# Scale copies tied to their transposes, first slots from nine tiles, one gather per f-tile, in a one-core attention and mixture-of-experts kernel

## The chip, the cores and the metric

The kernel runs on one core of a Trainium2 chip. The metric is the device time of one launch in microseconds; lower is better. Times of several runs are given as their median.

## What is computed

Linear attention (4 batch entries, 8 heads, 576 rows, 64 columns), then a dense gated feed-forward layer on the 2304 x 512 result, then a layer of 8 experts of which each row uses one:

```python
x = x @ w_gate * sigmoid(x @ w_gate) * (x @ w_val) @ w_out      # 512 -> 1536 -> 512
e_idx = np.argmax(x @ w_gate2, axis=1)                          # the row's expert
for e in range(8):
    mask = e_idx == e
    h = np.maximum(x[mask] @ w1[e], 0.0)                        # 512 -> 1024
    out[mask] = gate_w[mask, None] * eom[mask, e, None] * (h @ w2[e])
```

All of it is float32. The kernel splits every matmul operand into a high part and a low part and multiplies three times (high by high, high by low, low by high).

## The kernel before

The 2304 rows are 18 tiles of 128, handled by the dense layer in six blocks of 384 rows (three tiles). Blocks 0 to 3 run one after the other, mixed with attention. Blocks 4 and 5 share their first products in `pair` (lines 693 to 753). What is left of block 5 then runs alone: a loop over its 12 f-tiles (lines 1457 to 1474), here called **block 5's stretch**. For f-tile f it takes the low part of the hidden tile (`h5`, line 684, on VectorE), the split of the output weights (`cut`, line 641: the high part on ScalarE, the low part on GpSimd) and nine matmuls (`o_tiles`, line 577, trace lines 582 to 584). The third matmul of each group of three reads the hidden tile's low part. Every helper's instructions carry the helper's line, so `h5` and `cut` both show as L642 (ScalarE) and L643 (VectorE or GpSimd): 128x384 is a hidden tile, 128x512 are weights.

After a block, `post_x2` (line 909) writes its rows to the DRAM buffer `x2d`. `post(n)` (line 1366) lists what follows for block n: transposes (L920) with a copy back (L921), the logits (L928, L935), and the routing of its rows, `route_a` and `route_b`, the first of which writes each row's scale into four more columns of `x2d`. `route_early` (line 1037) and `slot_map` (line 1005) then pick rows for the first 8 slot tiles (two **quads** of four tiles, each with one expert) from the tiles known so far, `EARLY_T` = 12, which are blocks 0 to 3. These lists are worked off in small pieces between the large matmuls (`fine` during `pair`, `fill` later). Where the routing code goes through a recorder, its instructions show as L879 or, called directly, L876.

`rows` (line 1404) takes four gather buffers and `gather_q(0)` fetches the rows of the first quad by four indirect DMAs on GpSimd's queue (`fetch`, L1165). `xt_q(0, t)` (line 1193), called at f = 8 to 11, transposes gathered tile t on TensorE (L1179), copies the transpose's high part out on ScalarE (L1181), takes the low part on VectorE (L876) and copies the rows' scale to `SCQ` on VectorE (L1197). Then `quads` (line 1238) runs four quads; `split_q` (L1210, L1213) splits their weights. Single slots follow (`moe2`), four of them as long as the routing needs no more.

Within one engine instructions run in the order that a scheduler gave them. It may place an instruction far ahead of its place in the code as soon as its inputs are named as ready. `tie(x)` (line 901) bounds that: x is placed behind the last matmul kept in `state["pe"]`. It is an order, not a wait.

Of the kernel before, what the change touches and what calls it, by code (L numbers as in the profile page):

```python
# [19 lines left out]
P = 128  # L20
NT, DM, DFF = B * S, H * D, 1536
# [9 lines left out]
NEQ = 2  # L31
# [153 lines left out]
def kernel(ctx, tc, qT, kT, v1, wphi, w1cat, wlog, mw1, mw2, consts, out):  # L185
    nc = tc.nc
    PE, ACT, DVE, POOL, SP = nc.tensor, nc.scalar, nc.vector, nc.gpsimd, nc.sync
# [14 lines left out]
    def buf(n):  # L202
        a = ar.take(n)
        return A[:, a:a + n]
# [5 lines left out]
    o = 0  # L210
# [3 lines left out]
    ident = cv["ident"]  # L214
# [16 lines left out]
    SCQ = buf(8)  # L231
# [43 lines left out]
    state = {"n": 0, "banks": [0, 1, 2, 3, 4, 5, 6, 7], "rd": 0}  # L275
# [613 lines left out]
    def bc(ap, n):  # L889
        return ap.rearrange("p (j o) -> p j o", o=1).to_broadcast([P, ap.shape[1], n])  # L890

    def bm(ap, n):
        return ap.rearrange("p (o e) -> p o e", o=1).to_broadcast([P, n, ap.shape[1]])

    def v3(ap, j, e):
        return ap[:, :j * e].rearrange("p (j e) -> p j e", e=e)

    def tt(out_, a, b, op):
        return DV.tensor_tensor(out=out_, in0=a, in1=b, op=op)

    def tie(x):
        if x is not None:
            tc.add_manual_dep(x.ins, state["pe"].name, mybir.DependencyInfo(
                mybir.DependencyClass.NoSync, mybir.DependencyReason.SCHED_ONLY), reason="pace")

    def rsum(out_, a):
        DV.tensor_reduce(out=out_, in_=a, axis=AX.X, op=ALU.add)

    def post_x2(n, t):
        i = 3 * n + t  # L910
        x2 = X2[t]
        ACT.activation(x2, PS[:, (OUT5 if n == 5 else OUTB)[t], :], AF.Copy, scale=0.5)
        SP.dma_start(out=x2d[i * P:(i + 1) * P, 0:DM], in_=x2)
# [66 lines left out]
    def excl(out_, a):  # L980
        w = v3(T1, 8, 8)
        tt(w, cv["m8"].rearrange("p (e f) -> p e f", f=8), bm(a, 8), ALU.mult)
        rsum(out_, w)

    def pick(out_, a, nt):
        w = v3(T1, nt, 8)
        tt(w, OH[:, 0:nt, :], bm(a, nt), ALU.mult)
        rsum(out_, w)
# [40 lines left out]
        tt(T3[:, a:s0 + ns], EXF[:, a:s0 + ns], EXF[:, a - 2:s0 + ns - 2], ALU.not_equal)  # L1029
        DV.tensor_copy(CHI[:, a:s0 + ns], T3[:, a:s0 + ns])  # L1030

    EARLY_T = 12

    def every4(name):
        return cv[name][:, 3:16:4]

    def route_early():

        nt = EARLY_T
        q, tk, ge, r = S1[:, 0:nt], S2[:, 0:nt], S3[:, 0:nt], RK[:, 0:nt]  # L1040

        def counts():
            w = v3(T1, 8, 4)
            tie(tt(w, bc(NB, 4), bm(every4("thge"), 8), ALU.is_ge))
            rsum(E1, w)
            excl(E2, E1)

        def taken():
            tie(DV.tensor_scalar(out=E3, in0=E2, scalar1=-1.0, scalar2=float(NEQ), op0=ALU.mult, op1=ALU.add))
            DV.scalar_tensor_tensor(out=TKE, in0=E3, scalar=0.0, in1=E1, op0=ALU.max, op1=ALU.min)  # L1050
            tt(E4, E2, TKE, ALU.add)
            DV.tensor_scalar(out=TKE, in0=TKE, scalar1=4.0, scalar2=None, op0=ALU.mult)
            DV.tensor_scalar(out=E2, in0=E2, scalar1=4.0, scalar2=None, op0=ALU.mult)

        def picks():
            pick(q, E2, nt)
            pick(tk, TKE, nt)

        def place():
            tie(tt(ge, r, tk, ALU.is_ge))  # L1060
            tt(q, q, r, ALU.add)
            DV.scalar_tensor_tensor(out=q, in0=ge, scalar=1000.0, in1=q, op0=ALU.mult, op1=ALU.add)

        return [(totals, (nt,)), (counts, ()), (taken, ()), (experts, (E4, NEQ, 0)), (picks, ()),
                (place, ()), (slot_columns, (q, nt, 4 * NEQ, True))]
# [68 lines left out]
    XG = []  # L1134
# [28 lines left out]
    def fetch(col, i):  # L1163
        rows = EARLY_T * P if col < 4 * NEQ else NT
        return POOL.indirect_dma_start(out=XG[i], out_offset=None, in_=x2d[0:rows, :],  # L1165
                                       in_offset=IndirectOffsetOnAxis(ap=IDX[:, col:col + 1], axis=0),
                                       bounds_check=rows - 1, oob_is_err=False)
# [8 lines left out]
    def turn_x(i, hi, lo):  # L1176
        ps = PS[:, XB, :]
        for k in range(4):
            PE.transpose(ps[:, k * P:(k + 1) * P], XG[i][:, k * P:(k + 1) * P], ident)  # L1179
        p3 = ps.rearrange("p (k t) -> p k t", k=4)  # L1180
        ACT.activation(hi, p3, AF.Copy)  # L1181
        tt(lo, p3, hi.bitcast(F32), ALU.subtract)
# [1 line left out]
    def xt(s):  # L1184
        turn_x(s % 4, XCH[s % 2], XCL[s % 2])

    def gather_q(q):
        for t in range(4):
            g = fetch(4 * q + t, t)
            if q == 0:  # L1190
                tie(g)

    def xt_q(q, t):
        ts_ = slice(t * P, (t + 1) * P)
        turn_x(t, XQH[:, :, ts_], XQL[:, :, ts_])
        o = 4 * (q % 2) + t
        DVE.tensor_copy(SCQ[:, o:o + 1], XG[t][:, DM:DM + 1])  # L1197

    def split_q(g):
        q, c = divmod(g, 16)  # L1200
# [165 lines left out]
    def post(n):  # L1366
        return [(post_log, (n, t)) for t in range(3)] + [(f, (n,)) for f in (post_mm, post_sum, route_a, route_b)]
# [15 lines left out]
    def fine(n):  # L1383
        first = True
        while n > 0:
            if not small:
                if not todo:
                    return
                small.extend(ops(*todo.pop(0)))
                continue  # L1390
            e, f = small.pop(0)
            while True:
                x = f()
                if first and e in (DVE, ACT):
                    tie(x)
                    first = False
                if e is not PE or not small or small[0][0] is not PE:
                    break
                e, f = small.pop(0)
            n -= 1 if e is not None or f is idle else 2  # L1400
# [3 lines left out]
    def rows():  # L1404
        t = ov.tile([P, OVN], F32, name="ov_gather", tag="ov")
        for s in range(4):
            XG.append(t[:, s * 520:s * 520 + ROW])
            DVE.memset(XG[s], 0.0)
        gather_q(0)

    todo, xs = [], []
    for n in range(1, NBLK - 2):
# [30 lines left out]
    def rest(f, g):  # L1443
        if g == 2:
            if f == 0:
                for i in range(3):
                    post_x2(3, i)
                todo.extend(post(3) + route_early() + [(slot_map, (EARLY_T, 4 * NEQ, 0, True))])
        if f or g == 2:
            fine(2)  # L1450

# [5 lines left out]
    for f in range(NFT):  # L1457
        if f >= 2:
            h5(f)
        w = slot(3 * NFT + f)  # L1460
        cut(w, WR[f][2], POOL)
        mm = o_tiles(5, f, range(3), OUT5, G5(f), w)
        if f == 8:
            state["pe"] = mm.ins
        if f == 1:
            o_tiles(4, NFT - 1, range(3), OUTB, (GH[1], GL[1]), W2)
            for i in range(3):
                post_x2(4, i)
            load_w(0, 1)
            rows()  # L1470
        if f >= 2:
            fill(1)
        if f >= 8:
            xt_q(0, f - 8)
# [62 lines left out]
```

## Time and profile before

| what | us |
|---|---|
| time, median of 3 runs | 899.76 (899.32 to 900.19) |
| the profiled execution's own time | 898.41 |
| its span in the profile | 896.6 |
| TensorE busy in the span | 868.4 (97%) |
| mean granted clock | 0.992 |

The profile is of one execution. Its span runs from the first to the last instruction; the profiled execution's own time is 1.8 us longer, and 1.35 us under the median of the three runs. The granted clock is TensorE's, as a share of full speed. Times inside the trace are us from the span's start.

### The profile page before, as it was taken

The numbers are of one execution on the slowest core, as the hardware profiler recorded it, in microseconds if no ns is written. First come the engines' busy times: TensorE is split into PE (matmuls) and PEld (weight loads), VectorE is DVE, ScalarE is ACT, GpSimd is POOL, SyncE is SP. The second block draws the span as 40 slices with busy tenths as digits, with TensorE's granted clock in tenths as the row PEclk, the third lists the DMA queues.
The fourth block names the chain that finished last, engine by engine and source line by source line (L and its number), as shares of the span: only waits on it lengthen the run. The fifth ranks groups of instructions, "written<-read, shape, count | busy, mean of one in ns | idle before, by whom it ended". The sixth has DMA issues, their size and how long they took to land. (4 is left out here: it accounts for less than half of the span.)

```text
span 896.6 us, 17294 instructions
## 1 busy us (share of the span) xinstructions
PE 868.4 (97%) x6849; PEld 754.1 (84%) x6851; DVE 522.8 (58%) x1028; ACT 475.5 (53%) x921; POOL 387.2 (43%) x339
## 2 busy tenths in 40 slices
PE   8899999999999999999999999996999999999995
PEld 6789988989998988888899999995678888888784
DVE  6999785543335634546556676672677444344693
ACT  6867776535453544544465555562433434344783
POOL 1667989445543433443456566545301212120120
PEclk9999999999999999999999999998999999999998
DMA  8757544200020011110000000009411234010650
GB/s 239 225 174 219 164 129 133 63 16 1 2 77 17 27 43 43 28 51 1 1 2 1 36 1 1 1 4 361 137 41 27 75 112 165 17 55 1 225 215 11
DMA packets 20362, 70.41 MB, mean 79 GB/s; under 512 B 5294, under 2 KB 5550, under 8 KB 18992
## 3 DMA queue, kind: packets, MB, share of 16 engines
q1 hardware_dynamic: 16704, 59.21, 20.7%
q0 software_dynamic: 3200, 9.48, 3.3%
q8 instruction: 55, 0.90, 0.4%
q10 hardware_dynamic: 368, 0.53, 0.2%
q14 instruction: 35, 0.29, 0.1%
HBM read 72.84 MB, written 10.00 MB: 92 GB/s over the span
## 5 line engine op out<-in xcount | busy, mean ns | idle before, releaser
L529 POOL TENSOR_TENSOR arena_r<-arena,arena_r 128x512 fp32r<-128x512 f32 x143 | 184.3, 1293 | 176.0 <-ACT arena_r L525 175.8
L525 ACT ACTIVATE arena_r<-arena 128x512 fp32r<-128x512 f32 x143 | 90.1, 631 | 156.6 <-PE banks L546 96.8
L545 PE MATMUL banks<-arena_r 128*128 128x384 f32 x384 | 135.0, 352 | 0.0
L547 PE MATMUL banks<-arena_r 128*128 128x384 f32 x384 | 129.2, 336 | 0.0
L546 PE MATMUL banks<-arena_r 128*128 128x384 f32 x384 | 129.2, 336 | 0.0
L584 PE MATMUL banks<-arena_r 128*128 128x512 f32 x216 | 86.9, 402 | 7.9 <-DVE arena_r L643 7.9
L1210 ACT ACTIVATE arena_r<-arena 128x512 fp32r<-128x512 f32 x64 | 40.3, 632 | 97.8 <-PE banks L1221 46.9
L1213 DVE TENSOR_TENSOR arena_r<-arena,arena_r 128x512 fp32r<-128x512 f32 x64 | 45.1, 705 | 78.8 <-ACT arena_r L1210 78.6
L582 PE MATMUL banks<-arena_r 128*128 128x512 f32 x216 | 88.8, 411 | 0.0
L583 PE MATMUL banks<-arena_r 128*128 128x512 f32 x216 | 85.9, 398 | 0.0
L642 ACT ACTIVATE arena_r<-arena 128x512 fp32r<-128x512 f32 (+1 forms) x73 | 44.0, 612 | 64.9 <-PE banks L677 34.6
L545 PEld LDWEIGHTS banks<-arena_r 128*128 128x128 f32 x384 | 72.1, 188 | 5.0 <-issue 1.2
L546 PEld LDWEIGHTS banks<-arena_r 128*128 128x128 f32 x384 | 72.3, 188 | 0.6
L547 PEld LDWEIGHTS banks<-arena_r 128*128 128x128 f32 x384 | 72.1, 188 | 0.1
L1170 POOL DMA_INDIRECT out_dram<-arena x20 | 22.9, 1143 | 109.8 <-ACT arena L1265 39.1
L643 POOL TENSOR_TENSOR arena_r<-arena,arena_r 128x512 fp32r<-128x512 f32 x37 | 48.1, 1303 | 41.0 <-ACT arena_r L642 40.1
L557 DVE SCALAR_TENSOR_TENSOR arena<-arena,banks 128x384 f32<-128x384 f32 x48 | 26.5, 551 | 67.0 <-ACT arena L554 66.9
L1165 POOL DMA_INDIRECT ov_gather<-x2d,arena x20 | 21.7, 1086 | 99.1 <-PE banks L1179 96.5
L324 DVE TENSOR_REDUCE arena<-banks 128x6 f32<-128x768 f32 x48 | 45.8, 954 | 30.6 <-PE banks L316 29.7
L584 PEld LDWEIGHTS banks<-arena_r 128*128 128x128 f32 x216 | 41.2, 191 | 17.8 <-DVE arena_r L643 8.8
L316 PEld LDWEIGHTS banks<-arena 64*128 64x128 f32 x576 | 38.3, 187 | 16.8 <-issue 9.4
L1234 PE MATMUL banks<-arena_r 128*128 128x512 f32 x128 | 51.0, 399 | 0.0
(165 smaller groups left out, 2091.8 us busy)
## 6 DMA issues: line engine op xcount, KB each, us to landing
arena<-mw SPq DMA_DIRECT2D x16, 2048.0 KB, 8.0
ov_conv<-w1cat SPq DMA_DIRECT2D x24, 512.0 KB, 4.5
arena<-w1cat SPq DMA_DIRECT2D x12, 512.0 KB, 3.6
arena<-v SPq DMA_DIRECT2D x16, 325.0 KB, 3.3
x2d<-arena SPq DMA_DIRECT2D x18, 256.0 KB, 2.1
arena<-qT SPq DMA_DIRECT2D x15, 288.0 KB, 3.7
arena<-kT SPq DMA_DIRECT2D x15, 288.0 KB, 4.3
ov_gather<-x2d,arena POOLq DMA_INDIRECT x20, 3.7
```

The source lines that it names most:

```text
L324: DVE.tensor_reduce(out=MX, in_=ps, axis=AX.X, op=ALU.max, apply_absolute_value=True)
L525: ACT.activation(WH[i % 4], WR[f][w], AF.Copy)
L529: POOL.tensor_tensor(out=WL[i % 4], in0=WR[f][w], in1=WH[i % 4].bitcast(F32), op=ALU.subtract)
L545: PE.matmul(ps, wh[:, c], xh, start=(k == 0), stop=False)
L546: PE.matmul(ps, wh[:, c], xl, start=False, stop=False)
L547: state["pe"] = PE.matmul(ps, wl[:, c], xh, start=False, stop=(k == 3)).ins
L582: PE.matmul(ps, gh[:, ts_], woh, start=(f == 0), stop=False)
L583: PE.matmul(ps, gh[:, ts_], wol, start=False, stop=False)
L584: mm = PE.matmul(ps, gl[:, ts_], woh, start=False, stop=(f == NFT - 1))
L643: eng.tensor_tensor(out=w[1], in0=src, in1=w[0].bitcast(F32), op=ALU.subtract)
L1213: DVE.tensor_tensor(out=l, in0=src, in1=h.bitcast(F32), op=ALU.subtract)
L1234: PE.matmul(ps, h[:, c], wh, start=(f == 0), stop=False)
```

## The change

The scale copies are tied to their transposes, the first 8 slots are chosen from nine tiles (blocks 0 to 2), so that block 3's `post` can come after the choice, the memsets of the gather buffers are tied, and the four gathers of the first quad come one at a time behind f-tiles 2 to 5.

```diff
-    EARLY_T = 12
+    EARLY_T = 9
...
     def turn_x(i, hi, lo):
         ps = PS[:, XB, :]
         for k in range(4):
-            PE.transpose(ps[:, k * P:(k + 1) * P], XG[i][:, k * P:(k + 1) * P], ident)
+            mm = PE.transpose(ps[:, k * P:(k + 1) * P], XG[i][:, k * P:(k + 1) * P], ident)
+        state["pe"] = mm.ins
...
-    def gather_q(q):
-        for t in range(4):
-            g = fetch(4 * q + t, t)
-            if q == 0:
-                tie(g)
+    def gather_q(q, ts=range(4)):
+        for t in ts:
+            tie(fetch(4 * q + t, t))
...
-        DVE.tensor_copy(SCQ[:, o:o + 1], XG[t][:, DM:DM + 1])
+        tie(DVE.tensor_copy(SCQ[:, o:o + 1], XG[t][:, DM:DM + 1]))
...
-            DVE.memset(XG[s], 0.0)
-        gather_q(0)
+            tie(DVE.memset(XG[s], 0.0))
...
-                todo.extend(post(3) + route_early() + [(slot_map, (EARLY_T, 4 * NEQ, 0, True))])
+                todo.extend(route_early() + [(slot_map, (EARLY_T, 4 * NEQ, 0, True))] + post(3))
...
-        if f == 8:
-            state["pe"] = mm.ins
+        state["pe"] = mm.ins
+        if 2 <= f < 6:
+            gather_q(0, [f - 2])
```

What it moves, by engine. The lines of the changed kernel are one lower from `gather_q` on (L1197 becomes L1196), and L1181 becomes L1182.

VectorE, block 5's stretch, before: the scale copies (L1197) stand among the hidden tiles' low parts (L643) and the copies of block 4's transposes (L921).

```order
L643 TENSOR_TENSOR arena_r<-arena,arena_r 128x384 x2
L1197 COPY arena<-ov_gather 128x1 x2
L643 TENSOR_TENSOR arena_r<-arena,arena_r 128x384
L1197 COPY arena<-ov_gather 128x1
L921 COPY arena<-banks 128x512
L1197 COPY arena<-ov_gather 128x1
L643 TENSOR_TENSOR arena_r<-arena,arena_r 128x384
```

The same place in the changed kernel:

```order
L1407 MEMSET ov_gather 128x516 x4
L643 TENSOR_TENSOR arena_r<-arena,arena_r 128x384 x2
L921 COPY arena<-banks 128x512
L643 TENSOR_TENSOR arena_r<-arena,arena_r 128x384
L921 COPY arena<-banks 128x512
L643 TENSOR_TENSOR arena_r<-arena,arena_r 128x384
```

The scale copies are gone from here; each now stands next to the low part of its own transpose, some 25 rows later. The first two L643 of the first fence are f-tiles 2 and 3, the next are 4 and 5; in the second fence the first two are 3 and 4, and f-tile 5 follows one L921.

GpSimd, the same stretch: the gathers (L1165) against the low parts of the output weights (L643).

```order
-L643 TENSOR_TENSOR arena_r<-arena,arena_r 128x512 x6
-L1165 DMA ov_gather<-x2d,arena 128x516 x4
 L643 TENSOR_TENSOR arena_r<-arena,arena_r 128x512 x7
+L1165 DMA ov_gather<-x2d,arena 128x516
+L643 TENSOR_TENSOR arena_r<-arena,arena_r 128x512
+L1165 DMA ov_gather<-x2d,arena 128x516
+L643 TENSOR_TENSOR arena_r<-arena,arena_r 128x512
+L1165 DMA ov_gather<-x2d,arena 128x516
+L643 TENSOR_TENSOR arena_r<-arena,arena_r 128x512
+L1165 DMA ov_gather<-x2d,arena 128x516
+L643 TENSOR_TENSOR arena_r<-arena,arena_r 128x512 x3
```

Of seven weight splits (f-tiles 5 to 11) that stood behind all four gathers, f-tile 5's now stands ahead of them, and those of 6, 7 and 8 stand each behind one gather.

ScalarE, the end of the stretch and the start of the quads, in the changed kernel; in the kernel before, the first three L1210 (weights of the first quad) stood among the L1181.

```order
L1182 ACTIVATE arena_r<-banks 128x4x128
L642 ACTIVATE arena_r<-arena 128x384
L1182 ACTIVATE arena_r<-banks 128x4x128 x2
L912 ACTIVATE arena<-banks 128x512 x3
L1182 ACTIVATE arena_r<-banks 128x4x128
L1209 ACTIVATE arena_r<-arena 128x512 x4
```

The first quad's first three weight splits now come behind the last transpose's copy.

## Rows read from the trace of the kernel before

**Rows 1.** Page, 40 slices of the span: TensorE busy in tenths, granted clock.

```profile
PE   8899999999999999999999999996999999999995
PEclk9999999999999999999999999998999999999998
```

**Rows 2.** Waits of TensorE, whole span, longest: us in total, times, longest.

```profile
PE banks L584 <- DVE arena_r L643: 7.9, 2, 5.6
```

**Rows 3.** Timeline, TensorE: start, us, engine, line, operation, count, [idle before <-releaser].

```profile
612.80 0.60 PE L920 MATMUL banks<-arena 128*128 128x128 f32 x4
...
615.31 0.60 PE L920 MATMUL banks<-arena 128*128 128x128 f32 x4
...
615.98 0.40 PE L583 MATMUL banks<-arena_r 128*128 128x512 f32 x1
621.99 0.80 PE L584 MATMUL banks<-arena_r 128*128 128x512 f32 x1 [5.61 <-DVE arena_r L643]
...
625.25 0.81 PE L920 MATMUL banks<-arena 128*128 128x128 f32 x4
...
628.85 0.66 PE L584 MATMUL banks<-arena_r 128*128 128x512 f32 x1 [2.32 <-DVE arena_r L643]
...
632.00 1.04 PE L928 MATMUL banks<-arena 128*32 128x384 f32 x8
```

**Rows 4.** Timeline, VectorE, the same stretch.

```profile
621.29 0.15 DVE L1197 COPY arena<-ov_gather 128x1 f32<-128x1 f32 x1 [4.54 <-DMA ov_gather<-x2d,arena]
621.37 0.56 DVE L643 TENSOR_TENSOR arena_r<-arena,arena_r 128x384 fp32r<-128x384 f32 x1
...
628.15 0.15 DVE L1197 COPY arena<-ov_gather 128x1 f32<-128x1 f32 x1 [2.96 <-DMA ov_gather<-x2d,arena]
628.23 0.56 DVE L643 TENSOR_TENSOR arena_r<-arena,arena_r 128x384 fp32r<-128x384 f32 x1
```

**Rows 5.** Windows: stretch, length, busy time by engine, then granted clock, DMA share, GB/s.

```profile
622.00:625.20 3.20, 3.20 (x7) 2.13 (x7) 0.77 (x2) 0.25 (x1) 0.00 (x0) 0.50 0.93 392
```

**Rows 6.** Timeline, TensorE: routing's small matmuls at the pair's end.

```profile
606.04 0.45 PE L879 MATMUL banks<-arena 128*128 128x24 bf16 x12 [0.49 <-DVE arena L879]
606.34 0.48 PE L584 MATMUL banks<-arena_r 128*128 128x512 f32 x1
```

**Rows 7.** Timeline, TensorE, VectorE and ScalarE, from the transposes to the first quad.

```profile
639.74 0.61 ACT L1210 ACTIVATE arena_r<-arena 128x512 fp32r<-128x512 f32 x1
...
643.09 0.66 PE L1179 MATMUL banks<-arena,ov_gather 128*128 128x128 f32 x4 [0.25 <-DVE arena_r L876]
...
648.08 0.15 DVE L1197 COPY arena<-ov_gather 128x1 f32<-128x1 f32 x1 [2.06 <-DMA ov_gather<-x2d,arena]
...
648.88 0.66 PE L1179 MATMUL banks<-arena,ov_gather 128*128 128x128 f32 x4 [0.56 <-DVE arena_r L876]
...
650.22 0.73 PE L1220 MATMUL banks<-arena_r 128*128 128x512 f32 x2 [0.25 <-ACT arena_r L1181]
651.28 0.50 PE L1221 MATMUL banks<-arena_r 128*128 128x512 f32 x1 [0.33 <-DVE arena_r L876]
```

**Rows 8.** GpSimd: one weight split, all 20 gathers (ns min/median/max), all gathers to landing.

```profile
608.94 1.46 POOL L643 TENSOR_TENSOR arena_r<-arena,arena_r 128x512 fp32r<-128x512 f32 x1 [3.02 <-ACT arena_r L642]
...
L1165 POOL DMA_INDIRECT ov_gather<-x2d,arena x20: 995/1002/1612, 610.6 to 786.8; - x20
...
DMA to landing us min/median/max: 2.7/3.7/13.4
```

**Rows 9.** Timeline: stores to x2d on SyncE, a copy behind one; single slots' outputs.

```profile
610.22 1.90 SPq L913 DMA_DIRECT2D x2d<-arena  x3
...
647.60 1.71 SPq L913 DMA_DIRECT2D x2d<-arena  x3
...
652.23 0.69 DVE L921 COPY arena<-banks 128x512 f32<-128x512 f32 x1 [1.00 <-DMA x2d<-arena]
...
L1305 ACT ACTIVATE arena<-banks,ov_gather x4: 687/688/689, 855.2 to 887.4; 128x512 f32<-128x512 f32 x4
```

## The prediction

> **What bounds the kernel now.** I read the page's slices first. TensorE is busy in nearly every slice, and one slice stands out: the 28th of 40, about 605 to 627 us, at 6 tenths; in the slice behind it the granted clock falls [rows 1]. So TensorE sets the end, and only a gap of TensorE is worth anything. The table of waits names the gap: the matmul of L584, two waits, 7.9 us, released by VectorE's L643 [rows 2]. The timeline places both in block 5's stretch: L584 waits 5.61 us at 621.99 and 2.32 us at 628.85 [rows 3]. L584 is the matmul that reads the hidden tile's low part.
>
> Why was L643 late? On VectorE's timeline it starts at 621.37 right behind the scale copy L1197 of 621.29, which had itself waited 4.54 us for a gather to land; the second L643 (628.23) stands behind a copy that waited 2.96 us [rows 4]. The copies need 0.15 us and nobody needs them there. They stand ahead of the low parts of f-tiles 4 and 5 in VectorE's order, so TensorE waited for a gather it had no use for yet. Every gap has a second price: at 622.0 to 625.2 TensorE is busy all the time at a granted clock of 0.50, that is at 1.2 GHz instead of 2.4 [rows 5].
>
> **The change part by part.** *Copies behind their transposes.* The order of the changed kernel shows no scale copy among the low parts of f-tiles 2 to 8. I price this by starts on TensorE. With nothing in the way, transposes, nine matmuls and the next transposes take 615.31 - 612.80 = 2.51 us. The next two rounds took 625.25 - 615.31 = 9.94 and 632.00 - 625.25 = 6.75 us [rows 3]. Above 2.51 each that is 7.43 + 4.24 = **11.7 us**: 7.9 of waiting, the other 3.7 from the low clock. I expect both to go.
>
> *The routing's end.* The changed kernel makes the slot map during the pair and ends the pair with block 3's own ranking. Before, twelve small matmuls waited 0.49 us and ran from 606.04 to 606.34; six such, without a wait, should take half of the 0.30 [rows 6]. Gain 0.49 + 0.30 - 0.15 = **0.6 us**. Nine tiles instead of twelve also save three small matmuls, nothing that counts. Block 3's transposes move from the pair's start to its end, with as many rows as before; the pair's large matmuls cover them.
>
> *The transposes and the first quad.* Here TensorE waited 0.25, 0.56, 0.25 and 0.33 us [rows 7]. Three of the four were released by L876, the low parts of the transposes, behind scale copies of the next quad (one waited 2.06 us for its gather) and behind weight splits. Those 0.25 + 0.56 + 0.33 = 1.14 us should go, as the next quad's copies are tied too. Against this, the first quad's weight splits now come behind the last transpose's copy on ScalarE, and the first takes 0.61 us [rows 7], partly beside VectorE's last low part. I take a net gain of **0.7 us**; the ends are a loss of 0.6 (all of the split added, no wait gone) and a gain of 1.4 (all four waits gone).
>
> *Gathers between weight splits.* On GpSimd a split takes 1.46 us here, and a gather 1.0, the longest 1.61 [rows 8]; the splits of f-tiles 6, 7 and 8 now wait for one gather each, f-tile 9's for the fourth. From 608.94 + 1.46 = 610.4 on: f-tile 5's split to 611.9, then a gather and a split each round, at most 2.8 us with their gaps, so f-tile 8's ends at about 620.3 and f-tile 9's at 623. TensorE, at 2.51 us a round, reads them at 617.8 + 3 x 2.51 = 625.3 and at 627.9. Cost nothing, with 5 us of cover; gone when the four gathers take over 1.0 + 5 / 4 = 2.3 us each, and from there on every further us of a gather costs up to 4.
>
> *Will the gathers be there?* They start at about 612, 615, 618 and 620.5, later than before, but the transposes come earlier: without the gaps the first is due at 628.3 and the others 2.5 apart. The longest landing of any gather was 13.4 us (median 3.7) [rows 8], and those were issued under the same weight loads. By the worst, 620.5 + 13.4 = 633.9 against 635.8. Covered, by 2 us at the worst.
>
> *What now stands first on VectorE.* The low part of f-tile 5 comes behind the copy L921 of block 4's first transpose, which must wait until the store of these rows to `x2d` has landed. One such copy waited for its store until 652.23 [rows 9], 4.6 us after the first issue of its group at 647.6. Issued at 610.2 [rows 9], a store that slow is in by 614.8. TensorE's third matmul of f-tile 5 is due at 617.8 + 0.9 = 618.7 (0.9 from the round's L920 to it, as from 615.31 past 615.98 [rows 3]); less the copy, 0.69 [rows 9], and the low part, 0.56 [rows 4], the store must be in by 617.4. Covered, by 2.6 us. The memsets stay on VectorE and only close up.
>
> Sum: 11.7 + 0.6 + 0.7 = **13.0 us**. Against the profiled execution's own 898.4 that is 885.4; that execution is 1.35 us under the median of the runs shown, so on the median 899.76 - 13.0 = **886.8 us**.
>
> **The rivals.** *A late transfer takes the copies' place.* If the first store landed as slowly as the slowest gather, 610.2 + 13.4 = 623.6, the low part of f-tile 5 would be 6.2 us late at the same spot; if the last gather slipped by 5 us, TensorE would wait 3 at its transposes. For it: the DMA share is 0.93 while the weights load [rows 5], and the second quad's loads come earlier now, as the weights they overwrite are released earlier. Against it: stores are issued ahead of the weight loads, and each limit above used the worst row. Time: 3 to 6.2 us back and up to 2 of clock, 890 to 895. Chance 0.09.
>
> *Gathers that GpSimd builds slowly beside a busy VectorE.* Before, the four gathers were issued while VectorE stood idle; now it works. By rows the nearest is the longest of the 20, 1.61 us, with VectorE busy: below the 2.3 that decides, no loss. At 5 us each the four would cost 4 x (5 - 2.3) = 10.8 us, and 897.6 is the time. The Trainium skill speaks for it: "SBUF — State Buffer", section "SBUF: two separate sides", says that GpSimd cannot write the descriptors of its DMAs while VectorE holds the port pair that they share, and tells of a DMA that took about five times as long beside VectorE copies. By that factor, as an estimate from that page, a gather would take the 5 us just priced. The 1.61 us row [rows 8] does not agree with such a factor here, so the chance is 0.03.
>
> *Slower: an early quad runs empty.* The first two quads need two experts with at least 512 rows each among the first nine tiles (or one with 1024). If only one quad is filled, the other still runs, on nothing, and up to 512 rows come back as four more single slots. Four singles' outputs lie 887.4 - 855.2 = 32.2 us apart over three steps [rows 9], 10.7 each, so +43 - 13 = +30, about 930 us. Against it: nine tiles are 1152 rows, exactly two batch entries of 576, and with the reference's inputs each entry goes to one expert, 576 and 576, which fills the same two quads that twelve tiles fill. Chance 0.01.
>
> *The copies weren't it.* Each named wait could hide a second one that ends just after (a gap of L643 by ScalarE, say). ScalarE's high parts of these tiles were ready and the low part started 0.08 us after the copy [rows 4], so there is little room: 0.02, with a gain under 2 us.
>
> **How the numbers follow.** Forecast 0.85, late transfer 0.09, slow gathers 0.03, the copies weren't it 0.02, empty quad 0.01. The likeliest is the forecast, 886.8. Its own ends: the transposes' 0.6 loss instead of 0.7 gain gives 888.1, the 1.4 gain gives 886.1, and measuring against the profiled execution instead of the median gives another 1.4 down, 884.7. The range takes in the nearer end of the late transfer: 884.4 to 890.2. A measurement of this kernel tells 0.2% (1.8 us) from no change. Faster by more than that: forecast, late transfer and most of the slow gathers, 0.97; within it 0.015; slower 0.015.
>
> **What would show it.** In the changed kernel's waits, L584 behind L643 is gone; between the transposes L920 of block 5's stretch lie 2.5 us throughout, the granted clock stays 1.00 and no slice of TensorE falls to 6 before the last ones. The first L1179 starts some 12 us earlier, at about 627.8, and its gather has landed by then. VectorE has no wait for a gather ahead of an L643 of f-tiles 4 to 8. Wrong would be: L584 still waiting for L643, now with an L921 behind a store ahead of it; L1179 waiting for a gather; a weight split of GpSimd releasing L583; or more than four single slots.

## The result, and the profile after

The changed kernel takes **885.78 us** (median of 4 runs, 885.21 to 885.95), the kernel before 899.54 us beside it (4 runs, 899.03 to 900.19): a ratio of 0.9846, 95% interval 0.9828 to 0.9863. Predicted were 886.8 us, 884.4 to 890.2, a gain of 13.0; by the medians the gain is 13.8 us, by the two profiled executions 12.6. The profiled execution took 885.83 us with a span of 884.1; before, 898.41 and 896.6.

The page of the changed kernel, TensorE and its granted clock in 40 slices, to lay beside [rows 1]: the hole of the 28th slice and the fall of the clock in it are gone. (Both digits stand in the same slice of [rows 1]; the prediction read the fall into the slice behind.)

```profile
PE   8989999999999999999999999999999999999995
PEclk9999999999999999999999999999999999999998
```

The waits of TensorE in the changed kernel, the longest and the new one (us in total, times, longest). L584 [rows 2] no longer stands there; a new wait of 0.8 us ahead of the first quad does.

```profile
PE banks L387 <- DVE arena L327: 2.8, 4, 0.9
...
PE banks L1219 <- ACT arena_r L1209: 0.8, 1, 0.8
```

The timeline of TensorE over block 5's stretch, to lay beside [rows 3]. From L920 to L920 it is 2.51 and 2.52 us, and from the last L920 to L928 2.62; of these rounds the two with waits took 9.94 and 6.75 before.

```profile
613.14 0.60 PE L920 MATMUL banks<-arena 128*128 128x128 f32 x4
...
615.65 0.60 PE L920 MATMUL banks<-arena 128*128 128x128 f32 x4
...
618.17 0.60 PE L920 MATMUL banks<-arena 128*128 128x128 f32 x4
...
620.79 0.85 PE L928 MATMUL banks<-arena 128*32 128x384 f32 x8
...
628.73 0.64 PE L1179 MATMUL banks<-arena,ov_gather 128*128 128x128 f32 x4
...
638.19 0.50 PE L1219 MATMUL banks<-arena_r 128*128 128x512 f32 x1 [0.82 <-ACT arena_r L1209]
```

The timeline of VectorE, to lay beside [rows 4]: no scale copy stands ahead of the low parts any more, and the first one (now L1196) comes at 630.25 without a wait.

```profile
614.14 0.68 DVE L921 COPY arena<-banks 128x512 f32<-128x512 f32 x1
616.18 0.56 DVE L643 TENSOR_TENSOR arena_r<-arena,arena_r 128x384 fp32r<-128x384 f32 x1 [1.35 <-PE banks L584]
616.66 0.68 DVE L921 COPY arena<-banks 128x512 f32<-128x512 f32 x1
...
630.25 0.14 DVE L1196 COPY arena<-ov_gather 128x1 f32<-128x1 f32 x1
```

The windows of the changed kernel (stretch, length, busy time of TensorE, weight loads, VectorE, ScalarE, GpSimd; then granted clock, DMA share, GB/s), to lay beside [rows 5]: TensorE is busy all the time at a granted clock of 1.00, which is 2.4 GHz.

```profile
615.00:625.00 10.00, 10.00 (x56) 7.59 (x55) 3.81 (x8) 4.18 (x8) 7.56 (x8) 1.00 1.01 416
```

To see where the 12.5 us between the two spans lie, two more rows of the kernel before are wanted: a marker at the program's start and the first transposes of a gathered tile.

```profile
55.22 0.94 PE L316 MATMUL banks<-arena 64*128 64x128 f32 x12 [0.81 <-DVE arena L327]
...
640.12 0.64 PE L1179 MATMUL banks<-arena,ov_gather 128*128 128x128 f32 x4
```

In the changed kernel the marker stands at 55.65.

| Stretch | before | after | saved | predicted |
|---|---|---|---|---|
| start to the marker L316 | 55.22 | 55.65 | -0.43 | 0 |
| marker to the first L920 of block 5's stretch (pair, routing's end) | 557.58 | 557.49 | 0.09 | 0.6 |
| first L920 to first L1179 (block 5's f-tiles) | 27.32 | 15.59 | 11.73 | 11.7 |
| first L1179 to the end (transposes, quads, singles) | 256.48 | 255.37 | 1.11 | 0.7 |
| span | 896.6 | 884.1 | 12.5 | 13.0 |

The first line is scatter: over all the runs below the marker stands between 55.19 and 57.32 us, in programs that are alike up to there. The total came out right, the third line to 0.03 us. Whether the reason given for that line was right is another matter.

### The profile page after: what moved, and what is told of

It is laid out like the page before. It is cut to its first block, busy times and chain, and to the rows that moved or that the text cites. A ratio compares the mean times of both kernels' runs of the same rounds, so it can differ in the third digit from the quotient of the medians.

```text
span 884.1 us, 17277 instructions
## 1 busy us (share of the span) xinstructions
PE 864.3 (98%) x6846; PEld 752.7 (85%) x6848; DVE 526.7 (60%) x1028; ACT 474.6 (54%) x921; POOL 386.1 (44%) x339
## 5 line engine op out<-in xcount | busy, mean ns | idle before, releaser
L582 PE MATMUL banks<-arena_r 128*128 128x512 f32 x216 | 87.7, 407 | 0.0
L584 PE MATMUL banks<-arena_r 128*128 128x512 f32 x216 | 85.2, 394 | 0.0
L583 PE MATMUL banks<-arena_r 128*128 128x512 f32 x216 | 85.0, 393 | 0.0
L545 PEld LDWEIGHTS banks<-arena_r 128*128 128x128 f32 x384 | 72.1, 188 | 5.0 <-issue 1.3
L546 PEld LDWEIGHTS banks<-arena_r 128*128 128x128 f32 x384 | 72.3, 188 | 0.6
L547 PEld LDWEIGHTS banks<-arena_r 128*128 128x128 f32 x384 | 72.1, 188 | 0.1
L1165 POOL DMA_INDIRECT ov_gather<-x2d,arena x20 | 20.4, 1022 | 98.6 <-PE banks L1179 60.0
L643 POOL TENSOR_TENSOR arena_r<-arena,arena_r 128x512 fp32r<-128x512 f32 x37 | 48.1, 1299 | 29.9 <-ACT arena_r L642 28.9
L316 PEld LDWEIGHTS banks<-arena 64*128 64x128 f32 x576 | 38.3, 187 | 16.8 <-issue 9.7
L1219 PE MATMUL banks<-arena_r 128*128 128x512 f32 x128 | 50.2, 393 | 0.8 <-ACT arena_r L1209 0.8
L1233 PE MATMUL banks<-arena_r 128*128 128x512 f32 x128 | 51.0, 398 | 0.0
```

What stands on the lines that cost most here:

```text
L545: PE.matmul(ps, wh[:, c], xh, start=(k == 0), stop=False)
L546: PE.matmul(ps, wh[:, c], xl, start=False, stop=False)
L547: state["pe"] = PE.matmul(ps, wl[:, c], xh, start=False, stop=(k == 3)).ins
L582: PE.matmul(ps, gh[:, ts_], woh, start=(f == 0), stop=False)
L583: PE.matmul(ps, gh[:, ts_], wol, start=False, stop=False)
L584: mm = PE.matmul(ps, gl[:, ts_], woh, start=False, stop=(f == NFT - 1))
```

## The experiments

The median of the kernel before moves by 1 us from chip to chip (898.78 to 899.77), and the marker by 2 us between executions. So each ratio is to the kernel before on the same chip, and each run is also read by the interval from the first L920 of block 5's stretch to the span's end, which leaves the start out (TensorE's timeline, and the span). There is one trace of each run, and the interval scatters too: from the second quad's first transposes to the end, the changed kernel and the eight runs that don't differ from it there take 211.1 to 211.6 us. A difference of under some 0.5 us in the last column shows nothing by itself.

| Run | median, us | ratio to before, 95% | first L920 | span | interval | against the changed kernel |
|---|---|---|---|---|---|---|
| before | 899.54 | | 612.80 | 896.6 | 283.80 | +12.84 |
| the change | 885.78 | 0.9828 to 0.9863 | 613.14 | 884.1 | 270.96 | 0 |
| copies alone | 890.61 | 0.9887 to 0.9916 | 613.26 | 889.1 | 275.84 | +4.88 |
| all but the copies | 893.30 | 0.9918 to 0.9944 | 614.03 | 892.2 | 278.17 | +7.21 |
| twelve tiles | 885.99 | 0.9840 to 0.9868 | 613.09 | 883.9 | 270.81 | -0.15 |
| gathers together | 890.45 | 0.9883 to 0.9911 | 613.80 | 889.0 | 275.20 | +4.24 |
| together, low parts on VectorE | 885.89 | 0.9835 to 0.9868 | 612.69 | 883.4 | 270.71 | -0.25 |
| together, a shorter run | 887.91 | 0.9861 to 0.9895 | 613.79 | 886.4 | 272.61 | +1.65 |
| copies and low parts on VectorE | 887.50 | 0.9858 to 0.9897 | 614.01 | 885.5 | 271.49 | +0.53 |
| gathers late | 889.52 | 0.9868 to 0.9901 | 615.20 | 888.2 | 273.00 | +2.04 |
| splits behind f-tile 8 | 886.97 | 0.9840 to 0.9873 | 614.86 | 886.5 | 271.64 | +0.68 |
| splits behind f-tile 9 | 886.82 | 0.9846 to 0.9880 | 614.69 | 885.6 | 270.91 | -0.05 |
| transposes earlier | 886.77 | 0.9845 to 0.9878 | 612.97 | 884.2 | 271.23 | +0.27 |

### Which edit carries the gain?

**Copies alone.** The kernel before, with nothing but the scale copies tied behind their transposes (`tie` also takes the key of the matmul behind which it places x).

```diff
-            PE.transpose(ps[:, k * P:(k + 1) * P], XG[i][:, k * P:(k + 1) * P], ident)
+            mm = PE.transpose(ps[:, k * P:(k + 1) * P], XG[i][:, k * P:(k + 1) * P], ident)
+        state["turned"] = mm.ins
...
-        DVE.tensor_copy(SCQ[:, o:o + 1], XG[t][:, DM:DM + 1])
+        tie(DVE.tensor_copy(SCQ[:, o:o + 1], XG[t][:, DM:DM + 1]), "turned")
```

> The kernel before with one thing of the change: each scale copy is placed behind its own transposes. Theory (the copies alone held VectorE, and through it TensorE): both waits of L584 behind L643 go, the clock stays at full speed, and the time falls by 12 to 13 us, to 886.5 to 887.5, almost all of the whole change's 13.8. Rival (the change's gain comes from the earlier slot map and the spread gathers, the copies merely share it): a fall of under 8 us, over 891.

Measured: 890.61 us, a miss, about 3 us over what was expected. The copies are out of the way, and yet TensorE's timeline still has a wait of L584 for L643, one of 2.63 us where [rows 3] has 5.61 and 2.32:

```profile
622.00 0.50 PE L584 MATMUL banks<-arena_r 128*128 128x512 f32 x1 [2.63 <-DVE arena_r L643]
```

VectorE's L643 ahead of it took 5.64 us, where 0.56 is usual, and GpSimd's splits ran in one piece beside it:

```profile
616.30 5.64 DVE L643 TENSOR_TENSOR arena_r<-arena,arena_r 128x384 fp32r<-128x384 f32 x1 [1.35 <-ACT arena_r L642]
...
616.55 4.97 POOL L643 TENSOR_TENSOR arena_r<-arena,arena_r 128x512 fp32r<-128x512 f32 x4
```

So a second wait had stood behind the first one. Of the 12.84 us the copies alone bring 283.80 - 275.84 = 7.96. From the first L920 to the first L1179 they bring 7.30 of the 11.73: it takes 20.02 us here (633.28 - 613.26), 27.32 before and 15.59 in the changed kernel.

**All but the copies.** The changed kernel, with the copies free again.

```diff
-        tie(DVE.tensor_copy(SCQ[:, o:o + 1], XG[t][:, DM:DM + 1]))
+        DVE.tensor_copy(SCQ[:, o:o + 1], XG[t][:, DM:DM + 1])
```

> The changed kernel with the scale copies free again; the scheduler puts one behind each L921, ahead of the low parts of f-tiles 5, 6 and 7. Theory: those low parts wait for gathers once more. With the landings seen in the changed kernel (about 620, 624, 628 and 631) against needs of about 618, 620, 623 and 626, TensorE loses 4 to 6 us in waits and 1 to 3 to the low clock: 891 to 894. Rival (the gain is in the other edits): 886, as the changed kernel.

Measured: 893.30 us, as expected. The table of TensorE's waits shows VectorE late again, once at the low part and once at the copy of block 4's transposes, both behind scale copies that waited for their gathers:

```profile
PE banks L928 <- DVE arena L921: 3.3, 1, 3.3
...
PE banks L584 <- DVE arena_r L643: 1.8, 1, 1.8
```

The copies are needed, but not enough.

**Twelve tiles.** The changed kernel, with the slots chosen from twelve tiles and block 3's own ranking back ahead of the routing.

```diff
-    EARLY_T = 9
+    EARLY_T = 12
...
-                todo.extend(route_early() + [(slot_map, (EARLY_T, 4 * NEQ, 0, True))] + post(3))
+                todo.extend(post(3) + route_early() + [(slot_map, (EARLY_T, 4 * NEQ, 0, True))])
```

> The changed kernel with the first slots chosen from twelve tiles again, block 3's routing first. By the prediction's term for the routing's end it should be 0.6 us slower than the changed kernel (886.4). By the changed trace, where the pair itself grew by about what its end saved, it should be the same within 0.3 (885.5 to 886.1). Rival (nine tiles are what makes the gathers early enough): a wait for a gather at the transposes and 888 or more.

Measured: 885.99 us. The wait of [rows 6] is back on TensorE's timeline, with its 0.49 us, and costs nothing that can be measured: from the marker (55.57) to the first L920 (613.09) it is 557.52 us, against 557.49.

```profile
606.34 0.45 PE L879 MATMUL banks<-arena 128*128 128x24 bf16 x12 [0.49 <-DVE arena L879]
```

**Gathers together.** The changed kernel, with the four gathers one behind the other after f-tile 1, as before.

```diff
             tie(DVE.memset(XG[s], 0.0))
+        gather_q(0)
...
-        if 2 <= f < 6:
-            gather_q(0, [f - 2])
```

> The changed kernel with all four gathers behind f-tile 1, ahead of the weight splits of f-tiles 5 to 11, as before. Theory (the spread is worth nothing, GpSimd has some 5 us of cover): the same as the changed kernel within 0.3 (885.5 to 886.1), f-tile 5's split done by about 617 against a need of 618. Rival (splits behind four gathers come late): L583 waits for GpSimd's L643 by 1 us or more, 887 to 889.

Measured: 890.45 us, a miss: the spread of the gathers, to which the prediction gave nothing, is worth 4.24 us by the interval. The wait is the same as with the copies alone. VectorE's timeline of this run shows what TensorE waited for, in the second column: one L643 took 5.64 us.

```profile
614.33 0.56 DVE L643 TENSOR_TENSOR arena_r<-arena,arena_r 128x384 fp32r<-128x384 f32 x1 [1.01 <-PE banks L584]
...
616.84 5.64 DVE L643 TENSOR_TENSOR arena_r<-arena,arena_r 128x384 fp32r<-128x384 f32 x1 [1.12 <-PE banks L584]
```

Two instructions of one shape, one ten times as long as the other; the long one is not waiting for a semaphore, it is counted as busy. GpSimd's timeline of the same run tells what it shares those microseconds with:

```profile
616.07 1.00 POOL L1165 DMA_INDIRECT ov_gather<-x2d,arena  x1 [0.31 <-issue]
617.10 4.96 POOL L643 TENSOR_TENSOR arena_r<-arena,arena_r 128x512 fp32r<-128x512 f32 x4
```

While GpSimd issued four gathers in a row, four weight splits (f-tiles 5 to 8) queued up behind them, and then ran without a gap from 617.10 to 622.06. VectorE's L643 ended at 622.48. In the changed kernel GpSimd has the same splits and the same gathers, but by turns, and VectorE's L643 of 616.18 (0.56 us, above) falls into a gather's time:

```profile
614.24 1.29 POOL L643 TENSOR_TENSOR arena_r<-arena,arena_r 128x512 fp32r<-128x512 f32 x1 [1.49 <-ACT arena_r L642]
615.69 1.02 POOL L1165 DMA_INDIRECT ov_gather<-x2d,arena  x1 [0.16 <-issue]
616.76 1.29 POOL L643 TENSOR_TENSOR arena_r<-arena,arena_r 128x512 fp32r<-128x512 f32 x1
```

The price again has two parts. The round from L920 at 618.83 to L928 at 625.67 takes 6.84 us, against 2.62 in the changed kernel: 4.22 us more, of which 2.63 are the wait. Behind it TensorE is busy at a granted clock of 0.54, nearly all at 1.2 GHz (windows of this run):

```profile
622.50:625.60 3.10, 3.06 (x7) 2.00 (x7) 1.65 (x3) 0.24 (x1) 0.00 (x0) 0.54 1.02 430
```

### What makes one L643 ten times as long?

Theory: VectorE's two-input subtraction and GpSimd's subtraction can't both read SBUF at a time, and a run of GpSimd's without a gap keeps VectorE out until its end. Rival: the four gathers in a row do it, by their transfers or otherwise.

**Together, low parts on VectorE.** The gathers stay together; the run behind them is taken away. Against the kernel with the gathers together:

```diff
-        cut(w, WR[f][2], POOL)
+        cut(w, WR[f][2], DVE if 6 <= f < 10 else POOL)
```

> The changed kernel with all four gathers together behind f-tile 1 (the run of 890.45 us), and the low parts of block 5's weights of f-tiles 6 to 9 (four 128x512 subtractions, the run of 4.96 us on GpSimd right behind the gathers) computed on VectorE instead. In the run with the gathers together one subtraction of VectorE (L643, 128x384, usually 0.56 us) took 5.64 us, from 616.84 to 622.48, while GpSimd's four subtractions ran from 617.10 to 622.06 without a gap; TensorE then waited 2.63 us for it. Theory (two-input VectorE instructions and GpSimd's subtractions share a way to SBUF, and a run of GpSimd subtractions without a gap keeps VectorE out to its end): with GpSimd's four gone, VectorE's L643 take 0.56 us again, the wait of 2.63 us and its low clock are gone, and the time is 885.6 to 887.0 us. Rival (the four gathers standing together themselves hold VectorE or its operands up, by their transfers or their reads of the slot list): the long L643 and the wait stay, 889.5 to 891 us.

Measured: 885.89 us, as the theory has it, with the gathers as close together as before. VectorE does four more subtractions of some 0.7 us, and no wait for them stands on TensorE's timeline of block 5's stretch. The run of four turned out to be the splits of f-tiles 5 to 8, so one of GpSimd's was left, and VectorE's L643 shows just that one:

```profile
615.73 1.97 DVE L643 TENSOR_TENSOR arena_r<-arena,arena_r 128x384 fp32r<-128x384 f32 x1 [0.70 <-ACT arena_r L642]
```

Beside it on GpSimd:

```profile
614.95 1.00 POOL L1165 DMA_INDIRECT ov_gather<-x2d,arena  x1 [0.30 <-issue]
615.98 1.30 POOL L643 TENSOR_TENSOR arena_r<-arena,arena_r 128x512 fp32r<-128x512 f32 x1
```

**Together, a shorter run.** The same with `DVE if 8 <= f < 10`.

> The run with the four gathers together (890.45 us), with the weights' low parts of f-tiles 8 and 9 alone moved to VectorE, so that GpSimd's run behind the gathers is two subtractions of 1.24 us (2.5 us), not four. With four VectorE's L643 took 5.64 us, with one left it took 1.97 us. Theory (VectorE is kept out until GpSimd's run has ended, then does its 0.56 us): the long L643 takes 3.0 to 3.3 us and ends about 2.5 us earlier than in the run of four, at about 619.5 to 620.0 us, so that TensorE's wait of 2.63 us shrinks to 0 to 0.2 us: 885.6 to 886.6 us. Rival (VectorE is let in between GpSimd's instructions, and the 5.64 us had another cause, such as the gathers' own work): the L643 takes under 2 us or over 4 us, and the time doesn't follow the length of GpSimd's run.

Measured: 887.91 us. The number expected was missed, since the edit, counted by the same wrong f-tiles, left a run of three and not of two. By its letter the L643 of over 4 us is the rival's sign; but the rival had the time not follow the run's length, and it does follow. VectorE and TensorE of this run:

```profile
616.83 4.43 DVE L643 TENSOR_TENSOR arena_r<-arena,arena_r 128x384 fp32r<-128x384 f32 x1 [1.03 <-ACT arena_r L642]
```

```profile
621.31 0.50 PE L584 MATMUL banks<-arena_r 128*128 128x512 f32 x1 [1.42 <-DVE arena_r L643]
```

GpSimd's run here:

```profile
617.07 3.75 POOL L643 TENSOR_TENSOR arena_r<-arena,arena_r 128x512 fp32r<-128x512 f32 x3
```

Behind a run of 1, 3 and 4 subtractions (1.30, 3.75 and 4.96 us) the L643 takes 1.97, 4.43 and 5.64 us. Less the run that is 0.67, 0.68 and 0.68: always the run's length, and the instruction's own 0.56 us and 0.1 more with it. In none of these runs is VectorE let in between two of GpSimd's instructions. TensorE's wait follows: 0, 1.42, 2.63. That the gathers do it by themselves is out; they stood together in all three.

`pair` holds a comparison that needs no edit. In the changed kernel VectorE's L643, which reads both inputs from SBUF (`arena`, `arena_r`), takes 1.51 us beside a split of GpSimd; in the kernel before L696, of the same shape but with one input in PSUM (`banks`), takes its usual 0.56 in the middle of one:

```profile
605.77 1.29 POOL L643 TENSOR_TENSOR arena_r<-arena,arena_r 128x512 fp32r<-128x512 f32 x1 [0.80 <-ACT arena_r L642]
...
605.96 1.51 DVE L643 TENSOR_TENSOR arena_r<-arena,arena_r 128x384 fp32r<-128x384 f32 x1
```

```profile
600.31 1.29 POOL L643 TENSOR_TENSOR arena_r<-arena,arena_r 128x512 fp32r<-128x512 f32 x1 [2.17 <-ACT arena_r L642]
...
600.65 0.56 DVE L696 TENSOR_TENSOR banks<-arena,banks 128x384 f32<-128x384 f32 x1 [0.81 <-ACT arena L699]
```

So VectorE is not held up by everything it does beside a split of GpSimd; in these rows it is the instruction with both inputs in SBUF.

**Copies and low parts on VectorE.** The kernel before with two edits alone: the copies tied as above, and the weights' low parts of f-tiles 6 to 9 on VectorE.

> The kernel before with two edits alone: the scale copies tied to their own transposes (the run of 890.61 us), and the weights' low parts of f-tiles 6 to 9 on VectorE in place of GpSimd. The gathers stand together, twelve tiles choose the slots, and the routing is where it was. Theory (of the change's 13.8 us, the copies are worth 9 and the spread of the gathers about 4.5, that only by breaking GpSimd's run; the rest of the edits together under 0.5): 885.7 to 886.8 us. Rival (the spread has a worth of its own beside the run, or the routing's edits have): 887.5 to 890 us.

Measured: 887.50 us, 0.7 above what was expected and at the rival's edge. In this execution the marker stands at 56.49, 0.84 later than in the changed kernel; by the interval it is 0.53 us behind it. The f-tiles don't have them: from the first L920 to the first L1179 it takes 15.59 us (629.60 - 614.01), as in the changed kernel. A wait at the second transposes is back, as in [rows 7]:

```profile
632.66 0.66 PE L1179 MATMUL banks<-arena,ov_gather 128*128 128x128 f32 x4 [0.35 <-DVE arena_r L876]
```

But the wait of 0.82 ahead of the first quad is not there, and the quad starts 25.10 us behind the first L920, against 25.05. The difference lies in the first quad: from its start to the second quad's transposes it takes 35.20 us, against 34.48.

So block 5's 11.7 us are all gained without the spread, the nine tiles and the moved routing, if the copies are tied and GpSimd's run is broken in another way.

### Are the gathers there in time?

**Gathers late.** The changed kernel, with the gathers behind f-tiles 5 to 8.

```diff
-        if 2 <= f < 6:
-            gather_q(0, [f - 2])
+        if 5 <= f < 9:
+            gather_q(0, [f - 5])
```

> The changed kernel, with the four gathers behind f-tiles 5 to 8 in place of 2 to 5, about 8 to 10 us later, and the transposes where they are (due 628.7, 631.3, 633.8, 636.3 us). The gathers would be issued at about 620.7, 624, 627 and 630 us. In the changed kernel they land 8.6 to 10.4 us after their issue, while the 2 MB weight loads run. Theory (the landing takes as long wherever it is issued, so the slack of the gathers is only some 3 to 5 us): waits of L1179 for the rows add 1 to 4 us, 886.8 to 890 us. Rival (the landing is long only because of the weight loads that run beside it until about 626 us, and is 3 to 5 us behind them): within 0.5 us of the changed kernel, 885.3 to 886.3 us.

Measured: 889.52 us, as the theory expected; by the interval 2.04 us slower, and nearly all of that is the two new waits, 0.52 + 1.44:

```profile
631.45 0.65 PE L1179 MATMUL banks<-arena,ov_gather 128*128 128x128 f32 x4 [0.52 <-DMA ov_gather<-x2d,arena]
...
635.64 0.63 PE L1179 MATMUL banks<-arena,ov_gather 128*128 128x128 f32 x4 [1.44 <-DMA ov_gather<-x2d,arena]
```

The first gather was issued at 622.79 and the second at 625.56: 8.7 and 10.1 us until TensorE got their rows. The third and fourth landed faster, 7.5 and 4.6 us after their issue, so the rival had a part of it right. In the changed kernel the slowest gather of this stretch whose landing the trace has took 10.4 us; it is the fourth, issued at 620.71, so its rows were in by 631.1, and its transposes came at 636.34. The cover is real and is some 5 us.

```profile
DMA to landing us min/median/max: 5.1/9.2/10.4
```

### Is the 0.82 us ahead of the first quad worth taking away?

**Splits behind f-tile 8.** The first quad's weight splits tied to f-tile 8's products, as before the change (`tie(a, "f8")` in place of `tie(a)`).

> The changed kernel, with the first quad's three weight splits of ScalarE (L1209) tied again to the f-tile 8's products of block 5, not to the last transposes. In the changed kernel's trace these three run at 637.50 for 1.67 us, behind the last block's transposed copies and three evictions, and TensorE waits for them 0.8, 1.0 and 0.8 us (the first two overlapping the same start of the quad, the sum of the window from 635 to 640 being 4.18 of 5.00 us busy). Theory (the splits are what the quad's start waits for): 0.6 to 1.0 us faster than the changed kernel, 884.8 to 885.3 us. Rival (the quad's start waits just as long for the last transposed rows, L1182 at 637.03 and its low part behind it, so earlier splits buy nothing): 885.5 to 886.0 us. If the splits, now ahead of ScalarE's last high parts of block 5, wait there for the weights' transfer: slower than 886.

Measured: 886.97 us, 0.68 slower by the interval, which is hardly more than the scatter. Of the three waits named above, TensorE's timeline of the changed kernel has one, the 0.82 us. The quad does not start earlier against the first L920 (639.96 - 614.86 = 25.10 us, against 25.05), because the second transposes now wait. VectorE's timeline shows a subtraction of the early splits beside a split of GpSimd, 1.38 us instead of 0.69, and TensorE's the wait that comes of it:

```profile
630.74 1.38 DVE L1212 TENSOR_TENSOR arena_r<-arena,arena_r 128x512 fp32r<-128x512 f32 x1
```

```profile
633.51 0.66 PE L1179 MATMUL banks<-arena,ov_gather 128*128 128x128 f32 x4 [0.35 <-DVE arena_r L876]
```

**Splits behind f-tile 9**, where GpSimd has no split left.

> The changed kernel, with the first quad's three weight splits (L1209) tied to the products of block 5's f-tile 9: one f-tile later than in the run where they were tied to f-tile 8, which put VectorE's half of the first one beside GpSimd's last subtraction (1.38 us in place of 0.69) and made the second transposes wait 0.35 us. Behind f-tile 9 GpSimd has no subtraction left and ScalarE is idle about 2 us in each f-tile. Theory (the wait of 0.82 us before the quad is that for the splits, and nothing else collides): the quad's first product comes about 0.91 us behind the last row of evictions' transposes (L920) as in the run with f-tile 8, in place of 1.42, the interval from the first L920 of block 5's stretch to the quad's first product goes from 25.05 to about 24.5 us, and the time is 885.0 to 885.7 us. Rival (a wait returns at a transpose, as with f-tile 8): the interval stays at 25.0 or more and the time at 885.7 to 887 us. The start of the kernel scatters by about 1 us between executions, so the interval in the trace decides, not the time.

Measured: 886.82 us in an execution that began late (marker 56.75). Half of the theory came: the quad starts 24.65 us behind the first L920, 0.40 earlier, with one wait of 0.30. But the interval to the end is 270.91 us, the changed kernel's 270.96: the 0.40 us are lost again inside the first quad. The second quad's transposes come 34.99 us behind its start (674.33 - 639.34), against 34.48 (672.67 - 638.19). That is no scatter: in the seven runs that have these splits behind the last transposes the first quad takes 34.4 to 34.6 us, in the six that have them earlier, the kernel before among them, 34.9 to 35.2. Why, no row shows.

**Transposes earlier**, behind f-tiles 7 to 10 in place of 8 to 11.

> The changed kernel, with the four transposes of the first quad behind f-tiles 7 to 10, one f-tile (2.5 us) earlier, so that the last tile's transposed rows are there before block 5 ends, and the splits of the quad's weights are tied to an earlier product too. The gathers' rows are then due at about 626.2, 628.7, 631.3 and 633.8 us; in the changed kernel's trace they land at about 624.3 (second), 628.0 (third) and 631.1 (fourth), that is 3 to 4 us ahead of it at best and 0.7 us at worst for the second to the fourth shifted by one. Theory (the quad's start waits for its first operands, and the gathers are covered): 0.6 to 1.0 us faster, 884.8 to 885.3 us. Rival (a gather's rows come after their new due time and TensorE waits for them): 885.8 to 887 us, with a wait of L1179 for a DMA in the trace.

Measured: 886.77 us, 0.27 slower by the interval, which is within the scatter: the wait ahead of the quad is gone, one of 0.37 at the second transposes has come, again for L876 and not for a gather, and the first quad takes 35.01. None of the three beats the change.

## Why the prediction was right, and where its reasons weren't

- **Copies behind their transposes, 11.7 us.** The size is right (11.73), its cause only in part. Tied alone, the copies bring 7.30 us of it. The rest is a second wait of L584 for an L643 that ends 2.6 us later than TensorE wants it, and that the copies had hidden: with GpSimd's splits queued up behind four gathers, VectorE's low part runs ten times as long. The step that failed is "I expect both to go", said of the copies alone. The rival "the copies weren't it" had named the possibility of a second wait behind the first, looked for it on ScalarE, gave it a gain of under 2 us and a chance of 0.02.
- **Gathers between weight splits, "cost nothing".** Here the sign was wrong: by breaking GpSimd's run the spread earns 4.24 us by the interval. Both halves of the change are needed. The two errors cancel, because the change makes both edits; that the total came out is luck to that extent, since the prediction gave the spread no such worth. The prediction asked what the gathers do to GpSimd's splits, and not what the splits do to VectorE. The trace of before gave a hint. Of its L643 on VectorE, one of each shape is long without waiting for a semaphore: 1.32 us among the twelve of 128x384, where 0.54 to 0.56 is usual, and 1.81 among those of 128x512, where the usual is 0.69, both beside a split of GpSimd:

```profile
L643 DVE TENSOR_TENSOR arena_r<-arena,arena_r x36: 539/685/1806, 481.8 to 643.7; 128x512 fp32r<-128x512 f32 x24, 128x384 fp32r<-128x384 f32 x12
```

  and a run of three splits on GpSimd was there already, while VectorE stood idle behind a copy (the wait of [rows 4] that ended at 621.29):

```profile
615.77 3.72 POOL L643 TENSOR_TENSOR arena_r<-arena,arena_r 128x512 fp32r<-128x512 f32 x3
```

- **The routing's end, 0.6 us.** Mis-sized: 0.09 between marker and first L920, and with twelve tiles the wait is back at the same length of that stretch. The wait of 0.49 us goes, and block 3's transposes and ranking now stand elsewhere in the pair; that the pair loses there what its end saves fits the numbers, but no row shows where. A wait that goes is a gain only where its work doesn't come to stand on the same engine elsewhere.
- **The transposes and the first quad, 0.7 us.** Measured 1.11, inside its ends of -0.6 and 1.4. The four waits of [rows 7], 1.39 us in all, are gone, and the one that was foreseen, for ScalarE's splits behind the last transposes, has come with 0.82. Piece by piece, some 0.6 us of the gain lie ahead of the first quad and 0.7 in the quad itself (35.20 us before, 34.48 after), and 0.2 are lost again behind it, which is scatter. Of the 0.7 the one wait there, 0.33, is less than half; the rest was not foreseen and has no cause shown. None of the three runs got the 0.82 back.
- **The gathers in time.** Right: no L1179 waits, with about 5 us of cover where the prediction had 2 at the worst.
- **The head of VectorE's order.** Right: the first L921 runs at 614.14, without a wait for its store, and f-tile 5's low part is done at 616.74, 2.3 us before TensorE's third matmul of that f-tile (619.08).
- **"Every gap has a second price."** Not every one: behind the 1.42 us of the run of three the granted clock stayed at 1.00 (the last rows below).
- **Late transfer, slow gathers, empty quad.** None of them came. The gathers are issued in 995 to 1259 ns, and an L643 of VectorE falls into each of the first four; there are four single slots as before.

The rival of the slow gathers had GpSimd kept out by VectorE; what the runs show is VectorE kept out by GpSimd. The Trainium skill, "SBUF — State Buffer", section "Who interferes with whom", says that a VectorE instruction with two inputs in SBUF contends with a GpSimd instruction that reads SBUF, and that the one that loses stands still for the whole of the other. The rows of 1.97, 4.43 and 5.64 us agree with this; that what they contend for is a port, no run here shows. The page gives the shared pair to whichever starts first; by the recorded starts that was VectorE (616.84 against 617.10), and it was VectorE that was kept out. So the recorded starts don't tell who wins. In the run of the copies alone VectorE started 0.25 us ahead and was kept out (616.30 against 616.55); 7 us earlier it had started 0.24 us ahead and took its usual time, while GpSimd's split took 1.46 us in place of 1.3.

```profile
609.17 0.54 DVE L643 TENSOR_TENSOR arena_r<-arena,arena_r 128x384 fp32r<-128x384 f32 x1
...
609.41 1.46 POOL L643 TENSOR_TENSOR arena_r<-arena,arena_r 128x512 fp32r<-128x512 f32 x1 [3.03 <-ACT arena_r L642]
```

## What to carry to other kernels

When a wait is removed, look at what the waiting engine would have met, had it come on time: a run of instructions on another engine that was harmless while VectorE stood idle can be the next wait. A VectorE instruction whose duration is a multiple of its usual one, with no semaphore in it, can be a wait too. Here the table of waits put TensorE's wait down to VectorE and named GpSimd nowhere: compare the durations of one shape. Between GpSimd and VectorE, take turns: put GpSimd's DMA issues between its subtractions, or give VectorE a few of them.

## What the hardware did that wasn't expected

- A two-input VectorE subtraction of 0.56 us took 5.64 us beside four GpSimd subtractions in a row, and was not let in between them; beside one of GpSimd's gathers it took 0.56 us.
- The same 128x512 subtraction that takes GpSimd 1.24 to 1.30 us (1.46 to 1.65 where an L643 of VectorE had just begun) takes VectorE 0.68 to 0.69, so four of them moved over cost VectorE less than one blocked instruction.
- TensorE's clock did not fall behind every gap: after 1.42 us without work (the run of three) it was granted 1.00 in the window behind, after 2.63 us (the run of four) 0.54. The window of the shorter gap:

```profile
621.30:624.40 3.10, 3.09 (x17) 1.86 (x18) 3.07 (x6) 1.04 (x2) 0.00 (x0) 1.00 1.02 429
```
